# Attention and feed-forward on one core: the first eighteen feed-forward steps issued from one written list, the first eight attention units in pairs

## The chip, the cores and the metric

The kernel runs on one core of a Trainium2 chip. Its time is the device time of one execution in microseconds; the median of three runs is given. One further execution was profiled, and all rows below come from it. The engines are PE (matrix multiplication), DVE (vector), ACT (activation functions), POOL (general) and SP, which here only issues DMAs. Each works through its own queue in the order in which the program wrote it.

## What is computed

Attention over 4 batches, 8 heads, 768 positions and head size 64. A query sees the keys within 15 positions, and one summary per block of 32 keys (the maximum of the keys, the mean of the values). Then a feed-forward layer with weights of 512 x 2048 and 2048 x 512.

```python
k_sum = k.reshape(B, H, nb, block, D).max(axis=3)
v_sum = v.reshape(B, H, nb, block, D).mean(axis=3)
scores_l = np.where(abs(i - j) < 16, scale * q @ k.T, -1e9)
scores_s = scale * q @ k_sum.T + np.log(block)
a = softmax(concatenate([scores_l, scores_s]))
x = a @ concatenate([v, v_sum])          # heads side by side: 3072 x 512
h = x @ w_in                             # the weights come as 64-bit floats
g = h * np.tanh(log1p(exp(h)))           # Mish
out = g @ w_out
```

## The kernel before

**Attention.** 3072 tokens are cut into 12 chunks of 256 (three to a batch). A unit is one chunk and one pair of heads: 48 units, numbered in `todo` (L416) with the four head pairs of a chunk next to each other. For a unit, `att_products` (L282) multiplies queries with a window of 96 keys and 24 key summaries, `att_exponents` (L299) forms the maxima on DVE (L310) and the exponents on ACT (L315), `att_normalize` (L328) two reciprocals on DVE and a multiplication on POOL (L334), `att_transpose` (L336) four transposes on PE and a copy on ACT (L342), and `att_values` (L345) 16 products on PE (L361), the rounded upper half on ACT (xh, L363) and the rest on DVE (xl, L364).

**The first eight units** are chunks 0 and 1 (two chunks are one feed-forward group of 512 tokens). They use shared loads: `first_keys` (L201) all keys of a head pair and the queries of chunk 0, `more_queries` (L211) those of chunk 1, `first_values` (L218) the windows of chunk 0 and the rest of the values. `first_value_summary` (L232) gets the value means with eight products on PE (L239), a copy on ACT and a DMA that writes them beneath the windows (L243). Chunk 1 loads its windows as later chunks do (`att_load_values`, L264).

**Weights.** 16 tiles of two 512-column blocks, alternately from w_in and w_out, come as 64-bit floats and are made into an upper and a lower 32-bit part. `begin_weight` (L136) scales on ACT (L143) and shifts and masks on DVE (L144, L145); `join_weight` (L149) clamps (L154) and joins (L156) on DVE; `upper_weight` (L126) rounds on ACT; `lower_weight` (L131) subtracts on DVE (L134). The 64-bit tiles have two buffers, the float tile has one.

**Feed-forward.** 96 steps: six groups of 512 tokens by 16 blocks of 128 columns. `ff_in` (L370) is a block of twelve matmuls of 512 columns (ph), `ff_act` (L380) Mish on ACT, `ff_split` (L386) the halves ah (ACT in group 0, DVE later) and al (DVE), `ff_out` (L396) twelve matmuls (po). The output products of step i - 2 follow the input products of step i.

**The order.** The program text is the order (`manual_schedule`, L445). A loop over the first eight units (L459) does one unit a turn, with a quarter to a half of a weight tile in it. The loop over the steps (L499) follows: in group 0 one unit each one or two steps (L428) and a tile of weights each step, from group 1 on two units each four steps. Waits between engines come from the data.

Of the kernel before, what the change touches and what calls it, by code (L numbers as in the profile page):

```python
# [40 lines left out]
NR = (S - CH) // P  # L41
# [15 lines left out]
def fused_kernel(ctx: ExitStack, tc: tile.TileContext, q0, qk, kt, v0, vw, vs, w_in, w_out, out):  # L57
# [7 lines left out]
    small = ctx.enter_context(tc.tile_pool(name="small", bufs=4))  # L65
# [46 lines left out]
    loaded, begun, joined = [], [], []  # L112

    def load_weight():
        if weights:
            w, fc = weights.pop(0)
            t = stage.tile([P, WB, WP], I64, tag="stage", name=f"w{w}_{fc}")
            for k in range(WB):
                nc.sync.dma_start(t[:, k, :], (w_in, w_out)[w][fc + k])
            loaded.append((w, fc, t))  # L120

    def piece(w, part, fc):
        group, k = (early, fc) if fc < EARLY else (late, fc - EARLY)
        return group[w][part][:, k:k + WB, :].rearrange("p k f -> p (k f)")

    def upper_weight():  # L126
        if joined:
            w, fc, f = joined[0]
            nc.scalar.copy(piece(w, 0, fc), f)

    def lower_weight():  # L131
        if joined:
            w, fc, f = joined.pop(0)
            nc.vector.tensor_sub(piece(w, 1, fc), f, piece(w, 0, fc).bitcast(F32))  # L134

    def begin_weight():  # L136

        if loaded:
            w, fc, t = loaded.pop(0)
            words = t.rearrange("p k f -> p (k f)").bitcast(U32).rearrange("p (f two) -> p f two", two=2)  # L140
            x, high = words[:, :, 0], words[:, :, 1]
            f = ff.tile([P, WB * WP], F32, tag="f", name=f"w{w}_{fc}_f", bufs=1)
            nc.scalar.activation(f, high.bitcast(F32), AF.Copy, scale=2.0 ** -OFFSET)  # L143
            nc.vector.tensor_scalar(out=x, in0=x, scalar1=29, scalar2=None, op0=ALU.logical_shift_right)  # L144
            nc.vector.scalar_tensor_tensor(out=x, in0=high, scalar=SIGN, in1=x,  # L145
                                           op0=ALU.bitwise_and, op1=ALU.bitwise_or)
            begun.append((w, fc, f, x))

    def join_weight():  # L149

        if begun:
            w, fc, f, x = begun.pop(0)
            u = f.bitcast(U32)
            nc.vector.tensor_scalar(out=f, in0=f, scalar1=-_as_f32(F32_MAX), scalar2=_as_f32(F32_MAX),  # L154
                                    op0=ALU.max, op1=ALU.min)
            nc.vector.scalar_tensor_tensor(out=u, in0=u, scalar=3, in1=x,  # L156
                                           op0=ALU.logical_shift_left, op1=ALU.bitwise_or)
            joined.append((w, fc, f))
# [7 lines left out]
    blocks = first_att.tile([P, NQ + NR, NB], F32, tag="blocks", name="blocks", bufs=1)  # L166
    nc.gpsimd.memset(blocks, 1.0 / BLK)
    for part, step, at0 in ((blocks[:, :NQ], QT, -WIN), (blocks[:, NQ:], P, CH)):
# [7 lines left out]
    part = blocks[:, :NQ]  # L176
    nc.gpsimd.affine_select(
        out=part, in_=part, pattern=[[0, NQ], [0, NB]], base=-WIN, channel_multiplier=1,
        compare_op=ALU.is_ge, fill=0.0)
    nc.gpsimd.affine_select(  # L180
        out=part, in_=part, pattern=[[0, NQ], [0, NB]], base=WIN + QT - 1, channel_multiplier=-1,
        compare_op=ALU.is_ge, fill=0.0)


# [3 lines left out]
    rests = {}  # L188

# [11 lines left out]
    def first_keys(hp):  # L201

        ks = first_att.tile([P, WIN + S], F32, tag="ks", name=f"ks0_{hp}")
        nc.gpsimd.memset(ks[:, 0:WIN], 0.0)
        nc.sync.dma_start(ks[:, WIN:], kt[0, hp])
        t = first_att.tile([P, CG * CH], F32, tag="q0", name=f"q0_{hp}")
        nc.sync.dma_start(t[:, :CH], q0[hp])
        for c in range(CG):
            units[c, hp] = {"q": t[:, c * CH:(c + 1) * CH], "k": ks[:, c * CH:]}

    def more_queries(hp):  # L211

        t, other = units[1, hp]["q"], qk[1, hp].rearrange("p (s k) -> p s k", s=NQ)
        for h in range(2):
            r = slice(h * D, (h + 1) * D)
            nc.sync.dma_start(t[r].rearrange("p (s k) -> p s k", s=NQ), other[r, :, h * QT:(h + 1) * QT])

    def first_values(hp):  # L218
        vwt = first_att.tile([KA, NQ, P], F32, tag="vw", name=f"vw0_{hp}")
        nc.sync.dma_start(vwt[0:KW], vw[0, hp].rearrange("p (s k) -> p s k", s=NQ))  # L220
        t = first_att.tile([P, NR, P], F32, tag="v0", name=f"v0_{hp}", bufs=HP)
        nc.sync.dma_start(t, v0[hp].rearrange("p (j d) -> p j d", d=P))
        units[0, hp].update(v=vwt)
        rests[hp] = t

    def key_summary(b, hp, keys):
# [3 lines left out]
        summary[b, hp] = [km]  # L230

    def first_value_summary(hp):  # L232

        vm = att.tile([KA, P], F32, tag="vm", name=f"vm0_{hp}", bufs=HP)[KW:KA]
        summary[0, hp].append(vm)
        vwt, t = units[0, hp]["v"], rests.pop(hp)
        ps = att_psum(0, f"vm_ps0_{hp}")
        for j in range(NQ + NR):
            nc.tensor.matmul(ps[KW:KA, 0:P], *((blocks[0:KW, j, :], vwt[0:KW, j, :]) if j < NQ else  # L239
                                               (blocks[:, j, :], t[:, j - NQ, :])),  # L240
                             start=(j == 0), stop=(j == NQ + NR - 1))
        nc.scalar.copy(vm, ps[KW:KA, 0:P])
        nc.sync.dma_start(vwt[KW:KA], vm.unsqueeze(1).broadcast_to([NB, NQ, P]))  # L243

    def value_summary(b, hp):
        vm = att.tile([KA, P], F32, tag="vm", name=f"vm{b}_{hp}", bufs=HP)[KW:KA]
        summary[b, hp].append(vm)
        vq = att.tile([VP, BLK], F32, tag="vq", name=f"vq{b}_{hp}")
        nc.vector.reduce_sum(vq, sources.pop((b, hp, 1)), axis=AX.X)
        nc.vector.tensor_scalar_mul(vq, vq, 1.0 / BLK)  # L250
        nc.sync.dma_start(vm, vq)

    def att_load_keys(c, hp):
        b, th = divmod(c, CPB)
        if th == 0:
            key_summary(b, hp, sources.pop((b, hp, 0)))
            load_value_source(b, hp)
        km = summary[b, hp][0]
        t = att.tile([P, NQ, P + KA], F32, tag="qk", name=f"qk{c}_{hp}")
        nc.sync.dma_start(t, qk[c, hp].rearrange("p (s k) -> p s k", s=NQ))  # L260
        nc.gpsimd.tensor_copy(t[:, :, P + KW:], km.unsqueeze(1).broadcast_to([P, NQ, NB]))
        units[c, hp] = {"qk": t}
# [320 lines left out]
```

## Time and profile before

| what | us |
|---|---|
| median of three runs | 674.08 |
| range of the runs | 672.58 to 676.52 |
| the profiled execution | 672.3 |
| its span, first to last instruction | 670.6 |
| PE busy | 632.8 |
| DVE busy | 289.1 |
| ACT busy | 288.5 |
| POOL busy | 65.6 |

The span is what the profiler's rows cover; the time of the execution is a little longer than it. A busy PE means that a matmul is somewhere in its pipeline. [...]

### The profile page before, as it was taken

How to read it: one execution, taken by the hardware profiler on the slowest of the kernel's cores; microseconds unless marked ns; L12 is line 12 of the kernel's file. 1: busy time of each engine (PE TensorE's matmuls, PEld its weight loads, DVE VectorE, ACT ScalarE, POOL GpSimd, SP SyncE). 2: the span in 40 equal slices, each digit the busy share in tenths (PEclk: the TensorE clock that was granted, in tenths of full speed). 3: DMA queues.
4: the chain of work that ended last, by engine and by line, in shares of the span. 5: the costliest groups of instructions: out<-in, count | busy, mean ns of one | idle time of the engine just before them, and what ended most of it. 6: DMA issues, size and time to landing. Idle time of an engine off the chain costs nothing.

```text
span 670.6 us, 10932 instructions
## 1 busy us (share of the span) xinstructions
PE 632.8 (94%) x4224; PEld 515.0 (77%) x4224; DVE 289.1 (43%) x820; ACT 288.5 (43%) x674; POOL 65.6 (10%) x115
## 2 busy tenths in 40 slices
PE   4757979889999999999999999999999999999997
PEld 3645767667888888888888888888888888888886
DVE  3797889984242234552332344542332322322222
ACT  2686777777542442542442542442542442211111
POOL 3122001101101101101100100100100100000000
PEclk9877989899999999999999999999999999999999
DMA  8686446653231305361220225440340310000001
GB/s 277 172 261 212 157 166 233 234 169 116 77 111 43 114 1 163 109 189 43 91 64 27 91 87 162 120 131 29 99 129 16 91 31 1 36 27 1 0 1 63
DMA packets 32851, 69.53 MB, mean 104 GB/s; under 512 B 6944, under 2 KB 12064, under 8 KB 32800
## 3 DMA queue, kind: packets, MB, share of 16 engines
q1 hardware_dynamic: 32800, 68.84, 32.0%
q8 instruction: 33, 0.54, 0.3%
q14 instruction: 18, 0.15, 0.1%
HBM read 60.03 MB, written 6.29 MB: 99 GB/s over the span
## 4 chain that ended last, share of the span: by engine, by line
PE 80%; ACT 9%; DVE 5%; DMA 4%; issue 1%; SPq 0%
PE po L404 36%; PE ph L376 34%; PE x_ps L361 3%; PE sc L290 3%; PE pt_ps L340 2%; DVE w_f L156 2%; ACT w_f L143 2%; DVE w_f L154 2%; DMA vw<-vm 2%; ACT pr L315 1%; PE vm_ps L239 1%; DMA vw<-vw 1%; ACT L383 1%; ACT L315 1%; ACT a L383 1%
## 5 line engine op out<-in xcount | busy, mean ns | idle before, releaser
L383 ACT ACTIVATE a<-ph 128x512 f32<-128x512 f32 x96 | 57.5, 599 | 251.0 <-PE ph L376 158.0
L392 DVE CAST ah<-a 128x512 fp32r<-128x512 f32 x80 | 34.6, 433 | 234.4 <-ACT a L383 234.4
L404 PE MATMUL po<-w_early_out_hi,ah 128*128 128x512 f32 x240 | 97.3, 406 | 0.0
L376 PE MATMUL ph<-xh,w_early_in_hi 128*128 128x512 f32 x240 | 96.0, 400 | 0.0
L404 PE MATMUL po<-w_early_out_lo,ah 128*128 128x512 f32 x240 | 94.8, 395 | 0.0
L404 PE MATMUL po<-w_early_out_hi,al 128*128 128x512 f32 x240 | 94.5, 394 | 0.0
L376 PE MATMUL ph<-xl,w_early_in_hi 128*128 128x512 f32 x240 | 94.5, 394 | 0.0
L376 PE MATMUL ph<-xh,w_early_in_lo 128*128 128x512 f32 x240 | 94.3, 393 | 0.0
L334 POOL TENSOR_TENSOR pr<-pr,rs 128x480 f32<-128x480 f32 x48 | 48.2, 1003 | 396.7 <-DVE rs L333 365.3
L315 ACT ACTIVATE pr<-pr,nm 128x120 f32<-128x120 f32 x192 | 73.3, 383 | 10.0 <-DVE nm L310 9.7
L394 DVE TENSOR_TENSOR al<-a,ah 128x512 fp32r<-128x512 f32 x96 | 66.3, 691 | 2.8
L376 PE MATMUL ph<-xh,w_late_in_hi 128*128 128x512 f32 x144 | 57.1, 397 | 0.0
L404 PE MATMUL po<-w_late_out_hi,ah 128*128 128x512 f32 x144 | 57.0, 396 | 0.0
L404 PE MATMUL po<-w_late_out_lo,ah 128*128 128x512 f32 x144 | 56.2, 390 | 0.0
L376 PE MATMUL ph<-xh,w_late_in_lo 128*128 128x512 f32 x144 | 56.2, 390 | 0.0
L376 PE MATMUL ph<-xl,w_late_in_hi 128*128 128x512 f32 x144 | 56.1, 390 | 0.0
L404 PE MATMUL po<-w_late_out_hi,al 128*128 128x512 f32 x144 | 56.1, 389 | 0.0
L404 PEld LDWEIGHTS po<-w_early_out_hi,ah 128*128 128x128 f32 x240 | 45.8, 191 | 12.1 <-issue 2.8
L364 DVE TENSOR_TENSOR xl<-x_ps,xh 128x256 fp32r<-128x256 f32 (+1 forms) x32 | 17.8, 555 | 82.6 <-ACT xh L363 82.6
L404 PEld LDWEIGHTS po<-w_early_out_lo,ah 128*128 128x128 f32 x240 | 45.6, 190 | 10.0
L376 PEld LDWEIGHTS ph<-xh,w_early_in_lo 128*128 128x128 f32 x240 | 45.7, 190 | 9.7
L376 PEld LDWEIGHTS ph<-xh,w_early_in_hi 128*128 128x128 f32 x240 | 45.8, 191 | 9.5 <-issue 0.2
(74 smaller groups left out, 874.4 us busy)
## 6 DMA issues: line engine op xcount, KB each, us to landing
qk<-qk SPq DMA_DIRECT2D x40, 496.0 KB
vw<-vw SPq DMA_DIRECT2D x48, 192.0 KB
w<-w_in SPq DMA_DIRECT2D x16, 512.0 KB
w<-w_out SPq DMA_DIRECT2D x16, 512.0 KB
ks<-kt SPq DMA_DIRECT2D x17, 384.0 KB
out<-o SPq DMA_DIRECT2D x24, 256.0 KB
vsum<-vs SPq DMA_DIRECT2D x12, 384.0 KB
vw<-vm SPq DMA_DIRECT2D x48, 48.0 KB
```

What stands on the lines that cost most here:

```text
L143: nc.scalar.activation(f, high.bitcast(F32), AF.Copy, scale=2.0 ** -OFFSET)
L154: nc.vector.tensor_scalar(out=f, in0=f, scalar1=-_as_f32(F32_MAX), scalar2=_as_f32(F32_MAX), op0=ALU.max, op1=ALU.min)
L290: nc.tensor.matmul(ps[h][row, at0:at0 + KA], u["qk"][r, s, h * QT:(h + 1) * QT], u["qk"][r, s, P:], start=True, stop=True)
L315: nc.scalar.activation(pr[:, s, :], pr[:, s, :], AF.Exp, scale=-1.0, bias=nm[:, s:s + 1], accum_out=sm[:, s:s + 1])
L334: nc.gpsimd.tensor_mul(pr, pr, rs.unsqueeze(2).broadcast_to([P, NQ, KA]))
L361: nc.tensor.matmul(x, u["v"][:, s, d], pt, start=True, stop=True)
L364: return lambda: nc.vector.tensor_sub(xl, x, xh.bitcast(F32))
L376: nc.tensor.matmul(ph, w[:, cc * P:(cc + 1) * P], x[:, cc, :], start=(cc == 0 and n == 0), stop=(cc == NCC - 1 and n == 2))
L383: nc.scalar.activation(a, st[g, fc], AF.Mish)
L392: (nc.scalar.copy if g == 0 else nc.vector.tensor_copy)(ah, a)
L394: return lambda: nc.vector.tensor_sub(al, a, ah.bitcast(F32))
L404: nc.tensor.matmul(po[g][t], a[:, tok], w, start=(fc == 0 and n == 0), stop=(fc == NFC - 1 and n == 2))
```

## The change

Steps 0 to 18 of the feed-forward, all 16 weight tiles and units 0 to 19 are no longer issued by the two loops but by one list of 462 names, each a task of one to thirty-two instructions on one engine (or a few DMAs). The former functions are cut at engine borders into such tasks. The old loop over the steps starts at step 19 with the same work per step as before. Names used below: `S` scores of two units, `ttr` maxima, `exp` exponents, `rs` reciprocals, `nm` POOL's multiplication, `T` transposes, `pc` their copy, `X` output products, `xh`, `xl` the halves; `f`, `B`, `C`, `cl`, `E`, `hi`, `G` the seven operations of a weight tile in order; `ph`, `mi`, `ah`, `al`, `po` a step's; `km`, `vq` the key maxima and value sums; `l...` loads; `kc` POOL's copy of key maxima.

Besides the order:
- Chunks 0 and 1 of a head pair (`a`, `b`) get their scores and output products together: one `S`, one `X`, and one `xh` and `xl` of 512 columns.
- `first_queries` loads both chunks' queries at once, `first_values` both chunks' windows, and only the last 256 rows of the rest.
- The value means of the first batch are summed from the windows of both chunks (8 products) and the rest (2). They are not written beneath the windows by DMA any more: `X` begins each unit with two products of 256 columns with a tile `vm0`, whose first 96 rows are zero, and adds the windows' products to them.
- Small tiles have eight buffers instead of four. The first units' key, query and window tiles have three, the rest of the values two.
- Group 0's results are stored by `oc0` and `oc1` in the list.

```diff
+    def first_queries(hp):
+        t = first_att.tile([P, TG], F32, tag="q0", name=f"q0_{hp}", bufs=3)
+        nc.sync.dma_start(t[:, :CH], q0[hp])
...
+    def first_values(hp):
+        vwt = first_att.tile([KW, CG, NQ, P], F32, tag="vw", name=f"vw0_{hp}", bufs=3)
+        nc.sync.dma_start(vwt.rearrange("k c s d -> k c (s d)"), vw[0:CG, hp].rearrange("c k f -> k c f"))
...
     def first_value_summary(hp):
...
-        nc.scalar.copy(vm, ps[KW:KA, 0:P])
-        nc.sync.dma_start(vwt[KW:KA], vm.unsqueeze(1).broadcast_to([NB, NQ, P]))
+        nc.scalar.copy(vm, sums_ps.pop(hp)[KW:KA, 0:P])
...
     def att_values(*found):
...
+            rows = KW if c < CG else KA
+            if c < CG:
+                for h, d in enumerate(heads):
+                    nc.tensor.matmul(ps[d, k * CH:(k + 1) * CH], zeroed[hp][:, d],
+                                     u["pt"][:, h * NQ // 2:(h + 1) * NQ // 2, :], start=True, stop=False)
...
+    order = """
+        lk0 lk1 km1 km0 lqk8 lq0 S0 lq1 ttra0 S1 lk2 ttrb0 expa0 ttra1 lqk9 kc9 kc8 expb0 lw0 km2 rsa0 ttrb1 rsb0 S8
+        nma0 Ta0 lq2 nmb0 ttr8 lv0 expa1 expb1 S2 f0 B0 rsa1 C0 pca0 lv1 cl0 Tb0 lk3 lw1 ttra2 ttrb2 E0 exp8 rs8 lq3
+        expa2 nma1 pcb0 vm0 lv2 hi0 rsa2 ttr9 G0 km3 vm1 vc0 Ta1 nm8 B1 X0 T8 rsb1 S3 nma2 expb2 exp9 lvw8 vc1 lv3 C1 f1
+        nmb1 cl1 pca1 Tb1 rsb2 pc8 ttra3 E1 rs9 xh0 pcb1 vm2 ttrb3 lw2 X1 expa3 X8 hi1 xl0 G1 vc2 lqk11 nmb2 Ta2 nm9 Tb2
+        xh1 T9 xl1 expb3 lqk10 vm3 rsa3 nma3 pca2 pcb2 X2 xh8 ls12 lvw9 kc11 lw3 f2 Ta3 rsb3 B2 nmb3 C2 vc3 xh2 Tb3 kc10
+        pca3 xl8 cl2 E2 pcb3 hi2 S10 xl2 km12 ttr10 X3 pc9 xh3 X9 exp10 G2 xl3 ls13 ttr11 B3 lw4 ph0 f3 ph1 C3 exp11 ph2
+        cl3 xh9 mi0 E3 km13 xl9 hi3 ah0 rs10 ph3 mi1 lw5 ah1 B4 G3 al0 f4 C4 cl4 E4 mi2 al1 hi4 nm10 B5 G4 po0 mi3 f5 C5
+        lvw11 po1 T10 ph4 cl5 E5 lqk13 lqk12 lt12 hi5 vq12 ph5 ah3 ah2 al3 rs11 pc10 kc12 lw6 kc13 G5 f6 B6 nm11 ls15
+        lvw10 al2 C6 lw7 S12 mi4 cl6 E6 km15 X10 mi5 ttr12 ah4 hi6 xh10 lw8 G6 f7 T11 ttr13 po2 B7 po3 cl7 C7 exp12 E7
+        pc11 exp13 lt15 vq15 ph6 al4 hi7 B8 rs12 ah5 ph7 mi6 G7 dv12 al5 lqk14 nm12 po4 lw9 f8 ls14 ah6 po5 C8 xl10 X11
+        cl8 al6 E8 km14 hi8 lw10 mi7 lqk15 T12 rs13 G8 ah7 xh11 B9 lvw12 C9 f9 po6 cl9 nm13 lt13 E9 lw11 hi9 pc12 B10
+        al7 G9 kc15 f10 ph8 C10 mi8 xl11 ph9 cl10 po7 kc14 mi9 ah8 E10 S14 hi10 lw12 ah9 al8 ttr14 T13 ttr15 po8 G10
+        exp14 ph10 al9 vq13 f11 exp15 B11 dv13 mi10 C11 cl11 rs15 ph11 E11 ah10 po9 al10 hi11 B12 lqk16 G11 rs14 X12
+        mi11 ah11 lqk17 f12 pc13 C12 lt14 xh12 al11 nm15 cl12 lvw13 E12 po10 X13 hi12 xl12 kc16 T15 xh13 lw13 po11 vq14
+        lw14 dv14 G12 pc15 B13 ph12 f13 ph13 cl13 C13 xl13 mi12 E13 dv15 nm14 kc17 ah12 B14 T14 hi13 lvw15 mi13 S16 al12
+        lvw14 G13 ah13 lqk18 f14 lw15 al13 po12 X15 ttr16 C14 exp16 cl14 E14 rs16 ttr17 kc18 hi14 po13 pc14 X14 G14 ph14
+        B15 C15 exp17 nm16 xh14 xh15 xl15 rs17 nm17 f15 mi14 lvw17 xl14 cl15 E15 ph15 hi15 T17 ah14 lvw16 ph16 mi15 ah15
+        G15 al15 T16 ph17 pc17 al14 lqk19 kc19 X17 pc16 mi16 po14 po15 xh17 ah16 mi17 ah17 ph18 al16 oc0 oc1 mi18 X16
+        xl17 xh16 ah18 al18 xl16 lvw19 al17 lvw18 po16
+    """.split()
...
+    for k, word in enumerate(order):
+        name, what = parse(word)
+        ops[name](what)
...
-    for i in range(len(steps) + 2):
...
+    for i in range(done, len(steps) + 2):
```

## Rows read from the trace of the kernel before

**Rows 1.** Page, part 1: busy time of each engine, its share, instructions
```profile
PE 632.8 (94%) x4224; PEld 515.0 (77%) x4224; DVE 289.1 (43%) x820; ACT 288.5 (43%) x674; POOL 65.6 (10%) x115
```
**Rows 2.** Table by stage: busy us (x instructions), granted clock, DMA share, GB/s
```profile
core 0: us, PE busy (x) PEld busy (x) DVE busy (x) ACT busy (x) POOL busy (x), PEclk, DMA share, GB/s
4.40:55.67 51.27, 33.39 (x480) 26.34 (x480) 37.44 (x114) 29.93 (x92) 10.72 (x16) 0.83 0.81 245
55.67:150.40 94.73, 83.52 (x480) 63.65 (x478) 82.60 (x145) 68.75 (x120) 9.71 (x11) 0.93 0.56 191
...
193.10:670.60 477.50, 473.73 (x2985) 390.78 (x2983) 153.32 (x504) 163.20 (x403) 35.80 (x58) 1.00 0.22 71
```
**Rows 3.** Chain of waits in order of time: start us, us, what
```profile
55.74 4.45 PE ph L376 x12
...
197.88 2.95 PE po L404 x12
200.83 2.72 PE ph L376 x12
...
222.85 2.95 PE po L404 x12
```
**Rows 4.** Waits, 0 to 56 us: waiting line, releaser, us in total, times, longest
```profile
DVE pr L310 <- PE sc L296: 11.5, 6, 4.6
...
PE vm_ps L239 <- DMA vw<-vw: 5.1, 1, 5.1
...
PE sc L294 <- DMA q<-q: 4.5, 1, 4.5
...
PE x_ps L361 <- DMA vw<-vm: 3.4, 1, 3.4
```
**Rows 5.** Timeline of PE around step 19: start us, us, instruction
```profile
192.94 0.39 PE L376 MATMUL ph<-xh,w_early_in_hi 128*128 128x512 f32 x1
...
195.75 1.15 PE L361 MATMUL x_ps<-pt,vw 120*64 120x64 f32 x32
196.83 1.05 PE L290 MATMUL sc<-qk 64*64 64x120 f32 x32
```
**Rows 6.** Timeline of DVE, 99 to 108 us: a weight tile's operations
```profile
99.88 1.22 DVE L134 TENSOR_TENSOR w_early_out_lo<-w_f,w_early_out_hi 128x1024 fp32r<-128x1024 f32 x1
101.02 0.69 DVE L144 TENSOR_SCALAR w<-w 128x1024 uint32<-128x1024 uint32 x1
101.74 1.23 DVE L145 SCALAR_TENSOR_TENSOR w<-w 128x1024 uint32<-128x1024 uint32 x1
102.89 0.42 DVE L364 TENSOR_TENSOR xl<-x_ps,xh 128x256 fp32r<-128x256 f32 x1
103.53 0.69 DVE L154 TENSOR_SCALAR w_f<-w_f 128x1024 f32<-128x1024 f32 x1 [0.22 <-ACT w_f L143]
104.25 1.23 DVE L156 SCALAR_TENSOR_TENSOR w_f<-w_f,w 128x1024 uint32<-128x1024 uint32 x1
105.40 1.21 DVE L249 TENSOR_REDUCE vq<-vsum 96x32 f32<-96x1024 f32 x1
...
106.73 0.68 DVE L394 TENSOR_TENSOR al<-a,ah 128x512 fp32r<-128x512 f32 x1
107.33 1.21 DVE L134 TENSOR_TENSOR w_late_in_lo<-w_f,w_late_in_hi 128x1024 fp32r<-128x1024 f32 x1
```
**Rows 7.** Timeline of DVE: first of a unit's four maxima, and the next operation
```profile
42.54 0.28 DVE L310 CUSTOM_DVE_ANT_0 pr<-sc,base 128x120 f32<-128x120 f32 x1 [0.96 <-PE sc L296]
...
43.36 1.22 DVE L134 TENSOR_TENSOR w_early_in_lo<-w_f,w_early_in_hi 128x1024 fp32r<-128x1024 f32 x1
```
**Rows 8.** Table of 10 us pieces, columns as in rows 2
```profile
10.00:20.00 10.00, 8.33 (x70) 6.26 (x70) 5.35 (x16) 2.89 (x12) 0.98 (x1) 1.00 1.05 312
```
**Rows 9.** Waits, 60 to 160 us, columns as in rows 4
```profile
DVE w_f L154 <- ACT w_f L143: 4.2, 11, 0.6
```
**Rows 10.** Timelines of POOL and DVE at 143 us
```profile
143.65 0.99 POOL L334 TENSOR_TENSOR pr<-pr,rs 128x480 f32<-128x480 f32 x1 [7.35 <-ACT w_f L143]
...
143.69 1.50 DVE L154 TENSOR_SCALAR w_f<-w_f 128x1024 f32<-128x1024 f32 x1 [0.21 <-ACT w_f L143]
```

More of the change, by code (lines that the diff above doesn't have):

```diff
@@ L111, in fused_kernel @@
     weights = [(w, fc) for fc in range(0, NFC, WB) for w in range(2)]
[L112 to L158, printed above, removed]
+    raw, floats = {}, {}
@@ new lines, in load_weight, with words, piece @@
+    def load_weight(k):
+        w, fc = weights[k]
+        raw[k] = stage.tile([P, WB, WP], I64, tag="stage", name=f"w{w}_{fc}")
+        for j in range(WB):
+            nc.sync.dma_start(raw[k][:, j, :], (w_in, w_out)[w][fc + j])
+    def words(k):
+        t = raw[k].rearrange("p k f -> p (k f)").bitcast(U32).rearrange("p (f two) -> p f two", two=2)
+        return t[:, :, 0], t[:, :, 1]
+    def piece(k, part):
+        w, fc = weights[k]
+        group, j = (early, fc) if fc < EARLY else (late, fc - EARLY)
+        return group[w][part][:, j:j + WB, :].rearrange("p k f -> p (k f)")
@@ L188, in fused_kernel @@
     rests = {}
+    sums_ps = {}
+    means = {}
     sources = {}
@@ L347, in att_values @@
         n = len(found)
-        g, half = divmod(c, CG)
+        g = c // CG
         if g not in xs:
@@ new lines, in values_of, with upper_values, split_of, step @@
+    def values_of(name):
+        found = [(c, int(name)) for c in range(CG)] if int(name) < HP else [todo[int(name)]]
+        lowers[name] = att_values(*found)
+    def upper_values(name):
+        lowers[name] = att_rounded(*lowers[name])
+    def split_of(name):
+        lowers["a" + name] = ff_split(*steps[int(name)])
+    def step(f):
+        return lambda name: f(*steps[int(name)])
+    def number(f):
+        return lambda name: f(int(name))
+    def of_unit(f):
+        return lambda name: f(*unit(name))
@@ new lines, in fused_kernel, with parse, of_begin @@
+    """.split()
+    first_ops = {"lk", "lq", "lv", "vm", "vc"}
+    def parse(word):
+        name = next(m for m in sorted(ops, key=len, reverse=True) if word.startswith(m))
+        return name, word[len(name):]
+    def of_begin(word):
+        name, what = parse(word)
+        return name in first_ops or name in ("S", "ttr", "exp", "rs", "nm", "T", "pc", "X", "km") and (
+            what[0] in "ab" or int(what) < HP)
+    end_of_begin = max(k for k, word in enumerate(order) if of_begin(word))
@@ L420, in fused_kernel @@
+    ctx.enter_context(tc.manual_schedule())
+    for k, word in enumerate(order):
+        name, what = parse(word)
+        ops[name](what)
+        if k == end_of_begin:
+            begin.close()
+            late += weight_tiles(ctx.enter_context(tc.tile_pool(name="late", bufs=1)), "w_late", NFC - EARLY)
+    done = 1 + max(int(word[2:]) for word in order if word.startswith("ph"))
     scores, values, transposes, keys, sums, norms = ({} for _ in range(6))
@@ L426, in fused_kernel @@
         g, k = divmod(u - n, n)
-        if g == 0:
-            i = min(2 * k, 6 + k)
-            put(scores, i, u)
-            put(norms, i, u)
-            put(transposes, i + 1, u)
-            put(values, i + (3 if i < NFC - 4 else 2), u)
-            put(keys, i, u + 2)
-            put(sums, i + 1, u + 2)
-            continue
         pair, k = divmod(k, 2)
```

327 lines of the change are left out of this document (184 added, 143 removed).

## The prediction

> **What bounds the kernel now.** First the page's busy times: PE is busy 94% of the span, nothing else half [rows 1]. Then the table by stage [rows 2]: from 193 us to the end PE is never idle but for the last stores and its granted clock is 1.00, so nothing but removed PE work shortens that stretch, and the change removes none there. The loss is ahead of it. Up to 55.67 us, where the first feed-forward block begins [rows 3], PE is busy 33.4 of 51.3 us at a mean clock of 0.83; from there to 150.40 us it is busy 83.5 of 94.7 us. In that second stretch DVE is busy 82.6 of 94.7 us (87%): the weights' conversion sets the pace, and the 12.1 us in which DVE still waits are what a better order could win there. The waits of the first stage [rows 4] are latencies: DVE waits 11.5 us for score products, PE 5.1 us for the first value windows, 4.5 us for the first queries, 3.4 us for the value means' way through a DMA.
>
> So the whole change can be read from one mark, the start of block ph of step 19 (group 1, fc 3), since the list ends there and the loop behind it issues the same work as before. In the old kernel that mark is at 192.94 us [rows 5] and 477.66 us of the 670.6 us span lie behind it. The list has already done the output products of units 16 and 17, which the old kernel does behind the mark, in 1.08 us (195.75 to 196.83 us [rows 5]); 476.6 us remain. The new span is the new mark plus 476.6 us.
>
> **The price list.** A block of twelve 512-column matmuls takes 2.72 us [rows 3]. Four steps with two attention units take 222.85 - 197.88 = 24.97 us [rows 3], so a unit's scores, transposes and output products take (24.97 - 8 x 2.72)/2 = 1.6 us of PE, 0.53 us a piece. On DVE, from start to start [rows 6]: the five operations of a weight tile take 0.72 (B), 1.15 (C), 0.72 (cl), 1.15 (E) and 1.14 us (G), together 4.88 us; an al 0.60 us, a vq 1.33 us. The four maxima of a unit take 0.82 us (42.54 to 43.36 us [rows 7]). Three small kinds are estimates by size from the same rows: a key maximum reads 768 columns where vq reads 1024, 0.9 us; an xl 0.4 us as the one at 102.89 us (0.6 for 512 columns, as al); a pair of reciprocals of four columns 0.3 us.
>
> **Front, up to ph0.** ph0 waits for xl3, the last of the first eight units. In DVE's order the list puts ahead of it three weight tiles (14.6 us), the maxima of eleven units (9.0), five key maxima (4.5), ten reciprocals (3.0) and five xl (2.8): 33.9 us. DVE starts when the second keys have landed, about 5 us. Its waits: S0 now needs the queries of both chunks, and ahead of those stand two keys and the 0.5 MB block lqk8 in SP's order, 1.6 MB in all; at the 312 GB/s of 10 to 20 us [rows 8], counted from 2 us, and 1.5 us to land, that is about 8.6 us, against 4.5 us before (the wait for q from the span's start [rows 4]): some 2.5 us of DVE idle. S3 needs lq3, with 6.8 MB issued up to it: 2 + 21.8 + 1.5 = 25 us, and the 14.4 us of DVE work that the list puts from ttra3 to xl3 end at about 41 to 43 us. Adding a start at low clock (the first block, at 55.74 us, took 4.45 us where 2.72 is usual [rows 3]) I take ph0 at 45 us. Bounds: 42.5 us if DVE waits no more than 3.6 us, and 51 us if the loads run at the 245 GB/s that the first stage shows as its mean [rows 2] (6.8 MB then take 27.7 us, 6 us more). I take the value nearer to 10 to 20 us, since that is where loads are dense.
>
> Removed here: the DMA that copied the value means into each window tile (the 3.4 us wait and eight small transfers, and SP's time for them). Added on PE: sixteen 256-column products with the zero-padded means and eight more products in the value sums. No row has a 256-column plain f32 matmul; 16 output products of 64 columns are a third of a unit, 0.53 us or 33 ns each, so four times that is 0.13 us a piece and 2.1 us in all, and the upper end is a 512-column matmul's 0.227 us (2.72/12) doubled for halved packing, 7.3 us. I take 3 us: all of it is before ph0, where PE has some 25 us of work in 36 us (eight units at 1.6, eight pieces at 0.53, forty value sums at an estimated 0.13, and these 3), so it hides behind DVE; if that cover is gone it is added to ph0, and the 51 us bound holds it. [...]
>
> **From ph0 to ph14.** PE's order has 14 blocks ph and 14 po (76.2 us) and 18 pieces of units 10 to 16 (9.6 us): 85.8 us. DVE in the same part has twelve weight tiles (58.6), fourteen al (8.4), the maxima of seven units (5.7), four vq (5.3), three key maxima (2.7), seven reciprocals (2.1) and five xl (2.0): 84.8 us. The two are about equal, so every DVE wait over a microsecond moves PE. What is queued behind a wait is the rest of that engine's list, since the queues run in order; PE waits for G (a weight's lower half) and al. Where the old kernel waits 0.2 to 0.6 us eleven times for the scaling alone (4.2 us [rows 9]), the list puts other DVE work into these gaps: between E and G at least 1.1 us in all of tiles 3 to 14, against ACT's copy hi of about 1.05 us, and between G and the next cl at least 1.5 us in nine of eleven, against 1.15 us for the scaling (the exceptions are cl5 and cl13, with 1.15 and 0.73 us). So most of the 12.1 us goes. Bounds 0 and 12.1 us; I take 5 us, because ACT still has runs of exponents and table loads that delay a hi or f, and 1.7 us for the first block at low clock.
>
> POOL's multiplications and copies are as many as before. In the old trace one ran from 143.65 to 144.64 us, and the clamp L154 that began at 143.69 us took 1.50 us in place of 0.72 [rows 6, 10]: it ended 0.55 us after POOL. That is in my 5 us. [...]
>
> **Behind ph14** there is no weight to wait for but tile 15, done 6 us of DVE work later: eight blocks (21.8 us) and four pieces (2.1 us), 23.9 us at full clock. DVE's last entries hide behind that PE work; a missing al17 would cost the first loop step its length of 0.6 us.
>
> **The sum.** Mark = 45 + 85.8 + 6.7 + 23.9 = 161.4 us; span 161.4 + 476.6 = 638.0 us. The profiled run of before took 672.3 us, 1.7 us more than its span, and the median of the three runs is 674.08 us, 1.8 us above that. The same on top gives 641.5 us, a gain of 32.6 us (4.8%).
>
> **The rivals.**
> 1. DVE waits as before: the order only trades one wait for another, and DVE keeps its 12.1 us of idle per 94.7 us. 7.1 us more than I take: 648.6 us. For it: ACT is in order too, and a hi behind two exponents comes late. Against: the filled gaps. The same price comes from POOL, if each of the seven multiplications between ph0 and ph14 holds DVE for its full 0.99 us [rows 10]: 6.9 us.
> 2. A late front: SP issues in order, and lv3 waits for a window buffer that X0 frees, with lw2 behind it; or loads at 245 GB/s. ph0 at 51 us: 647.5 us; with rival 1 together 654.6 us.
> 3. Everything fits: ph0 at 42.5 us and 2 us of waits (the clock among them): 634.3 us.
> 4. The clock stays low: if the list scatters PE's idle time so that blocks run as the first one did [rows 3], each of the 36 costs 4.45 - 2.72 = 1.73 us more. From 19 such blocks on the gain is gone; all 36 give 641.5 + 62 = 704 us. Against: the old trace has 0.93 in the stretch from 55.67 us although PE is idle 12% of it [rows 2].
> 5. The list wins nothing: waits that the durations of one run could not foresee eat 30 us, 672 us. That would need DVE idle 2.5 times as long as now, in gaps that the list fills.
>
> **How the numbers follow.** Forecast (636 to 646 us) 0.52; rival 1 0.20; rival 2, alone or with 1, 0.13; rival 3 0.10; rival 4 0.03; rival 5 0.02. From 632 us (nearly all of rival 3) to 656 us (both of 1 and 2) leaves out the tails and rivals 4 and 5. A measurement of this kernel can tell about 0.5% (3.4 us) from no change: faster 0.95, within 0.02, slower 0.03.
>
> **What would show it.** Right: ph0 near 45 us; PE without idle gaps over 1 us from there on; DVE over 93% busy from ph0 to the last weight's lower half; that last G at about 140 us (149 us before); step 19's ph at about 161 us; from it on a profile like the old one, 476 to 477 us long. Wrong: ph0 beyond 51 us with DVE waiting for DMA (rival 2); DVE under 88% with waits for ACT (rival 1); PEclk under 0.9 behind ph0 (rival 4); or a part behind the mark that is not the same length, which would break the whole reading.

## The result, and the profile after

The changed kernel took 647.12 us (median of four runs, 646.79 to 647.77), the kernel before 674.79 us beside it (672.58 to 676.52): ratio 0.959, 95% interval 0.956 to 0.962. The forecast was 641.5 us. The execution profiled below took 647.03 us, its span is 645.3 us. "Front" is what lies ahead of ph0 (the first feed-forward block), "the mark" the start of block ph of step 19, as in the prediction. The list issues steps 0 to 18, nineteen in all.

Page, part 1, of the kernel after, which answers to [rows 1]:

```profile
PE 626.7 (97%) x4272; PEld 510.5 (79%) x4272; DVE 288.8 (45%) x817; ACT 270.5 (42%) x659; POOL 75.0 (12%) x119
```

The table by stage of the kernel after, cut at its own ph0, near the last weight tile, and at the mark; columns as in [rows 2], the granted clock as a share of full speed:

```profile
0.00:46.75 46.75, 34.04 (x633) 29.27 (x633) 35.14 (x132) 31.66 (x106) 20.21 (x45) 1.00 0.91 256
46.75:138.00 91.25, 89.25 (x558) 71.11 (x555) 88.97 (x163) 65.78 (x135) 17.58 (x14) 1.00 0.67 227
138.00:162.19 24.19, 24.19 (x135) 19.42 (x135) 12.54 (x21) 10.59 (x18) 1.45 (x2) 1.00 0.30 96
162.19:645.30 483.11, 479.26 (x2953) 390.70 (x2951) 152.11 (x503) 162.48 (x402) 35.76 (x58) 1.00 0.22 69
```

Read it from the top. ph0 is at 46.75 us instead of 55.7 us. From there DVE is busy 88.97 of 91.25 us (97.5%; 87% in [rows 2]) and PE 89.25. PE then runs without a gap to the mark at 162.19 us, 30.75 us earlier than the 192.94 us of [rows 5]. The last line is the surprise: the stretch behind the mark, where the clock is 1.00 and PE waits for nothing but the last stores, takes 483.11 us where 476.6 us were expected.

The timeline of PE at the mark, and the chain of waits behind it, which answer to [rows 5] and [rows 3]:

```profile
162.19 0.39 PE L422 MATMUL ph<-xh,w_early_in_hi 128*128 128x512 f32 x1
```
```profile
191.33 2.98 PE po L450 x12
194.31 2.77 PE ph L422 x12
197.08 2.79 PE po L450 x12
...
216.73 3.00 PE po L450 x12
219.72 2.78 PE ph L422 x12
```

A block of twelve matmuls takes 2.77 to 2.79 us where it took 2.72 us, and four steps take 216.73 - 191.33 = 25.40 us instead of 24.97 us. No wait shows and the clock is full: the matmuls themselves stand further apart.

### The profile page after: what moved, and what is told of

The parts are those of the page before. It is cut to its first block, busy times and chain, and to the rows that moved or that the text cites. A ratio compares the mean times of both kernels' runs of the same rounds, so it can differ in the third digit from the quotient of the medians.

```text
span 645.3 us, 10991 instructions
## 1 busy us (share of the span) xinstructions
PE 626.7 (97%) x4272; PEld 510.5 (79%) x4272; DVE 288.8 (45%) x817; ACT 270.5 (42%) x659; POOL 75.0 (12%) x119
## 4 chain that ended last, share of the span: by engine, by line
PE 80%; DVE 6%; ACT 1%; issue 1%; DVEq 0%
PE po L450 37%; PE ph L422 36%; PE x_ps L398 3%; PE sc L312 2%; PE pt_ps L371 2%; DVE w L140 1%; DVE al L440 1%; DVE w L136 1%; DVE w_f L144 1%; DVE w_f L149 1%; DVE w_early_out_lo L157 1%; ACT pr L345 0%; DVE vq L260 0%; DVE km L239 0%; DVE pr L334 0%
## 5 line engine op out<-in xcount | busy, mean ns | idle before, releaser
L365 POOL TENSOR_TENSOR pr<-pr,rs 128x480 f32<-128x480 f32 x48 | 54.8, 1143 | 362.2 <-DVE rs L361 297.3
L440 DVE TENSOR_TENSOR al<-a,ah 128x512 fp32r<-128x512 f32 x96 | 68.1, 710 | 4.0 <-ACT ah L438 1.3
L450 PE MATMUL po<-w_late_out_hi,al 128*128 128x512 f32 x144 | 56.2, 390 | 0.0
L450 PEld LDWEIGHTS po<-w_early_out_hi,al 128*128 128x128 f32 x240 | 45.3, 189 | 10.4 <-DVE al L440 0.5
L422 PEld LDWEIGHTS ph<-xl,w_early_in_hi 128*128 128x128 f32 x240 | 45.2, 188 | 9.5
```

Of the source, the lines that this page charges most:

```text
L365: nc.gpsimd.tensor_mul(u["p"], u["p"], u["r"].unsqueeze(2).broadcast_to([P, NQ, KA]))
L422: nc.tensor.matmul(ph, w[:, cc * P:(cc + 1) * P], x[:, cc, :], start=(cc == 0 and n == 0), stop=(cc == NCC - 1 and n == 2))
L440: return lambda: nc.vector.tensor_sub(al, a, ah.bitcast(F32))
L450: nc.tensor.matmul(po[g][t], a[:, tok], w, start=(fc == 0 and n == 0), stop=(fc == NFC - 1 and n == 2))
```

## The experiments

The rows of each kernel are cut at its own ph0 and mark. The distance between the starts of successive matmuls inside a block, behind the mark, is worked out from the trace's start times ("early" weights are fc 0 to 9, "late" 10 to 15, each kind some 300 to 500 distances; those over 300 ns, at block starts behind attention products, are left out); the last column is the first 512-column matmul behind the mark to the last.

| kernel | ph early | po early | ph late | po late | us |
|---|---|---|---|---|---|
| before | 227.0 ns | 227.3 | 227.3 | 227.0 | 473.50 |
| after | 228.8 | 232.9 | 232.6 | 228.0 | 478.87 |
| four buffers | 227.0 | 227.4 | 227.3 | 227.0 | 472.45 |
| four buffers and 384 bytes | 228.8 | 232.9 | 232.6 | 227.9 | 478.87 |
| old kernel, eight buffers | 229.0 | 232.9 | 232.6 | 228.0 | 480.03 |
| four buffers and 128 bytes | 228.8 | 232.9 | 232.6 | 227.9 | 478.87 |
| four buffers, 32 and 224 bytes | 227.2 | 232.8 | 227.2 | 232.9 | 478.23 |

The old kernel's last column holds the 1.08 us of units 16 and 17 that the list does ahead of the mark.

Two things limit what one profile of each kernel can tell. The runs come from three chips, on which the kernel before took 672.58, 673.68 and 672.58 us, so differences of about 1 us between runs of different chips say nothing. And the list with its tasks unchanged stands in five profiles (after, four buffers, and the three with unused tiles): their ph0 is at 46.75, 45.04, 45.62, 44.44 and 44.58 us. A shift of ph0 inside these 2.3 us is no effect by itself.

**One: the small tiles.** The only part of the change that touches the loop behind the mark is the line on the small tiles. Eight buffers instead of four make that pool 384 bytes larger in each partition, and what is allocated behind it (ah, al, the late weights) moves up by 384 bytes, while the early weights, xh and xl stay.

```diff
-    small = ctx.enter_context(tc.tile_pool(name="small", bufs=8))
+    small = ctx.enter_context(tc.tile_pool(name="small", bufs=4))
```

> The changed kernel with four buffers for the small tiles in place of eight, nothing else. That also moves ah, al and the late weights 384 bytes down, to where they lay in the old kernel. Theory A (address): the blocks behind step 19 take 2.78 us in place of 2.72 because, since the change, the two operands of a matmul start at different distances from a 512-byte border (32 for early weights and x, 416 for ah, al and late weights); here all start at 32 again, blocks are 2.72 us, the stretch behind step 19 is 476.6 us instead of 483.1, and the time is 640.5 us. Theory B (the list leaves something behind: order, semaphores, waits): 483 us and 647 us, unchanged. Theory C (fewer buffers bring waits in the first 50 us): the mark moves later than 162.2 us by 1 us or more.

Measured: 639.89 us (638.83 to 640.78), ratio 0.951 (0.950 to 0.953). This version beats both kernels. Its table by stage:

```profile
0.00:45.04 45.04, 33.47 (x632) 28.68 (x632) 35.20 (x132) 31.60 (x106) 20.21 (x45) 1.00 0.90 266
45.04:136.00 90.96, 88.80 (x542) 71.32 (x538) 88.39 (x162) 64.66 (x129) 17.34 (x14) 0.98 0.68 228
136.00:161.10 25.10, 25.10 (x153) 20.38 (x153) 13.80 (x22) 11.76 (x24) 1.81 (x2) 1.00 0.29 93
161.10:637.90 476.80, 472.88 (x2953) 390.05 (x2952) 152.72 (x503) 162.41 (x402) 35.73 (x58) 1.00 0.23 70
```

Behind the mark 476.80 us for the same 2953 records: the prediction's 476.6 us. The list doesn't need the eight buffers: DVE is as busy from ph0 on (88.39 of 90.96 us) as with them.

**Two: the addresses, not the buffers.** Four buffers, and an unused tile of 384 bytes in the same place.

```diff
+    pad = small.tile([P, 96], F32, name="pad", bufs=1)
+    nc.gpsimd.memset(pad[:, 0:1], 0.0)
```

> As the run before, with four buffers, and an unused tile of 384 bytes per partition behind them, so that ah, al and the late weights lie where the changed kernel has them. Theory A (address): 2.78 us blocks again, 483 us behind step 19, 647 us. If the number of buffers did it: 476.6 us and 640.5 us as with four buffers.

Measured: 645.69 us, 5.8 us more than its neighbour on the same chip, and 478.87 us in the table above, to the hundredth the changed kernel's. So the cost is the place of the operands.

**Three: the old kernel with the same line.** In the kernel before, only the small tiles' buffers go from four to eight.

```diff
-    small = ctx.enter_context(tc.tile_pool(name="small", bufs=4))
+    small = ctx.enter_context(tc.tile_pool(name="small", bufs=8))
```

> The old kernel with eight buffers for the small tiles and nothing else of the change: ah, al and the late weights move up by 384 bytes. Theory A (address): the old kernel gets the slow blocks, 484.1 us behind step 19 in place of 477.7 us, and 6.5 to 8 us more in all, 681 to 682 us. Theory B (the list): no change, 674 us, 226.7 ns from matmul to matmul.

Measured: 678.22 us beside 672.58 us, ratio 1.008 (1.006 to 1.010). The direction held, the size didn't: behind the mark it loses 6.5 us (473.50 to 480.03 us), but its mark stays where it was (193.1 us). Ahead of it PE waits for the weights anyway [rows 2], and slower matmuls can hide in those waits; that is argued, not shown.

**Four: another distance.** As in the second, with 128 bytes.

```diff
+    pad = small.tile([P, 32], F32, name="pad", bufs=1)
...
```

> Four buffers and an unused tile of 128 bytes: ah, al and the late weights start 160 bytes behind a 512-byte border, the early weights and x 32. Theory A in the form that any different distance costs: 483 us behind step 19. In the form that only some distances collide: 476.6 us, or a size between.

Measured: 646.75 us (two runs, 644.71 to 648.80), the same 478.87 us. By the kernels' allocation all these operands begin at 32 modulo 512 bytes in the old kernel and with four buffers. In the changed kernel ah, al and the late weights begin at 416, here at 160. Slow are the products whose two operands begin at different places (po early, ph late); po late, with both operands moved alike, costs 1 ns. (ph early, with neither operand moved, loses 1.8 ns here. Cut by place in the block, the loss lies in the first seven distances of the blocks that follow a po early block, 231.1 ns in the mean; from the eighth on they are back at 226.9 ns. So the slow block ahead reaches into them; how isn't shown.) So it is the distance between stationary and moving operand that counts, not where they lie.

**Five: which distances.** 32 unused bytes ahead of ah, 224 more ahead of the late weights.

```diff
+    pad = small.tile([P, 8], F32, name="pad", bufs=1)
...
+    pad2 = more.tile([P, 56], F32, name="pad2")
...
```

> The list with small tiles in four buffers (639.89 us, all matmul spacings behind step 19 at 227.0 to 227.5 ns), with two unused tiles: one of 32 bytes ahead of ah and al, one of 224 bytes between them and the late weights. The start addresses modulo 512 bytes are then 32 for the early weights, xh and xl, 64 for ah and al, 288 for the late weights; so the operands of a product differ by 0 (ph early), 32 (po early), 256 (ph late) and 224 (po late). Theory, any difference modulo 512 costs: po early, ph late and po late at 231 to 233 ns, about 6 to 7 us behind the mark, 646 to 648 us. Rival, the period is 256 bytes: ph late stays at 227.2 ns. Rival, only differences of 64 bytes or more cost: po early stays at 227.5 ns.

Measured: 644.39 us. Of the two products per group that are moved, po early (32 bytes apart) and po late (224) take 232.8 and 232.9 ns, ph late, 256 bytes apart, 227.2 ns. "Any difference modulo 512" fell; differences of 0 and 256 bytes cost nothing, and 32, 128, 224 and 384 bytes cost about the same 5.6 ns (2.5%). Distances under 32 bytes weren't tried.

**Six: what sets the pace from ph0 on.** The sign operation of each weight tile left out.

```diff
-        x, high = words(k)
-        nc.vector.scalar_tensor_tensor(out=x, in0=high, scalar=SIGN, in1=x,
-                                       op0=ALU.bitwise_and, op1=ALU.bitwise_or)
+        return
```

> The list with small tiles in four buffers (the kernel of the first experiment, 639.89 us, ph0 at 44.8 us, step 19 at 160.9 us, 477 us behind it), and the sign operation of each weight tile (1.15 us of DVE, 16 of them, 18.4 us in all) left out; so the weights lose their sign and the output is wrong. It asks which engine sets the pace of the list. Theory, as the prediction has it (front set by DVE, from ph0 on DVE and PE about equal, 84.8 against 85.8 us): ph0 comes up to 3.4 us earlier (three tiles), at 41.4 to 43 us; from ph0 to the mark little more is won, 0 to 3 us, as PE has 110 us of work in these 116 us; span 3 to 6 us shorter, 634 to 637 us. Rival, DVE alone sets the pace: 3.4 us in front and half or more of the other 14.9 us, 9 us or more, 629 us or less. Rival, PE alone sets it, in the front too (its scores wait for loads): under 2 us, 638 us or more.

Measured: 637.30 us (635.63 to 637.87), ratio 0.947 (0.943 to 0.950). Its table by stage, the first two lines cut at its ph0:

```profile
0.00:44.80 44.80, 34.80 (x632) 29.93 (x632) 31.16 (x129) 31.30 (x106) 17.53 (x45) 0.92 0.87 273
44.80:136.00 91.20, 90.65 (x571) 73.43 (x568) 76.50 (x156) 68.89 (x139) 14.25 (x15) 1.00 0.70 229
44.80:157.20 112.40, 111.85 (x693) 90.51 (x690) 85.38 (x169) 76.40 (x152) 14.52 (x16) 1.00 0.62 203
```

Some 12 us of DVE's work less from ph0 to 136 us, and the mark comes 3.9 us earlier (the medians differ by 2.6 us): PE is at its limit there (90.65 of 91.20 us). Of the 3.7 us won behind ph0, 1.6 us is idle time of PE that went. Another 1.7 us is a low clock that this execution didn't have: with four buffers PE waits 1.94 us for a window, and the row of 65 to 75 us shows a clock of 0.83 (0.50 from 72 to 74 us; before the wait PE had worked at 1.00). 10 us at 0.83 cost 1.7 us (10 x 0.17, an estimate).

```profile
65.00:75.00 10.00, 8.06 (x73) 6.54 (x72) 9.60 (x21) 5.91 (x10) 1.81 (x1) 0.83 0.64 189
```
```profile
70.97 1.12 PE L398 MATMUL x_ps<-pt,vw 120*64 120x64 f32 x16 [1.94 <-DMA vw<-vm]
```

The changed kernel has the same wait (1.79 us) and kept 1.00, so this part is one execution's.

In front, three operations (3.4 us) less left ph0 at 44.8 us, inside the spread of the unchanged lists. This doesn't yet show that the front isn't DVE's sum, because the clock differs too (0.92 up to ph0, 1.00 with nothing cut):

```profile
14.80:21.40 6.60, 6.10 (x80) 5.02 (x81) 5.64 (x31) 6.60 (x29) 2.03 (x3) 0.51 1.06 297
18.00:44.83 26.83, 26.83 (x434) 22.61 (x427) 21.84 (x79) 22.30 (x71) 8.73 (x10) 0.94 0.85 270
```

6.10 us of PE's work at a clock of 0.51 cost some 3 us (6.10 x 0.49, an estimate), about what DVE was spared, and from 18 us on PE ran to ph0 without a gap. In this execution PE held the front; what the cut is worth at full clock isn't shown.

**Seven and eight: what sets the front.** PE's value sums cut to a fifth, and then both cuts together.

```diff
-        for j in range(NW + NR):
+        for j in range(NW, NW + NR):
...
```

> The list with four buffers, and of the value sums of the first four head pairs only the products with the rest of the values (sixteen of the twenty matmul records, 1.9 us of PE, left out for each head pair, 7.4 us in all before ph0; the value means are wrong). The previous experiment, 3.4 us less of DVE's work in the front, left ph0 at 44.8 us (45.0 with it), and PE's queue there ran without a gap from 16.4 us on. Theory now: PE's own work sets the front as much as DVE's: ph0 1 to 5 us earlier, 635 to 639 us. Rival, as the prediction had it, DVE's work alone sets it: ph0 within 0.5 us, 639.4 to 640.4 us. Rival, the loads set it (90% DMA share up to ph0): the same, within 0.5 us.

> Both cuts: the value sums as in the run before and the sign operation of each weight tile left out (the values and the weights' signs are wrong). Theory, PE and DVE are both near the front's length: ph0 4 to 7 us earlier than 45.0 us, as neither holds it any more, and step 19 7 to 10 us earlier than 161.1 us, 630 to 633 us. Rival, the loads hold the front: ph0 not more than 1 us earlier and 636 to 638 us, as without the sign alone.

Measured: 637.98 us with ph0 at 43.8 us, and 635.48 us with ph0 at 43.3 us. The two cuts put ph0 1.2 and 1.7 us earlier than with four buffers and nothing cut, where 1 to 5 and 4 to 7 us were expected; that is 0.6 and 1.1 us under the earliest of the unchanged lists. The first time lies in its range, the second misses its 630 to 633 us. The front of the second, from 16 us to its ph0, and the same stretch with four buffers and nothing cut:

```profile
16.00:43.30 27.30, 22.95 (x408) 17.93 (x406) 23.67 (x90) 25.03 (x79) 11.18 (x12) 0.89 0.99 277
```
```profile
16.00:45.04 29.04, 26.88 (x468) 22.60 (x468) 27.79 (x89) 24.68 (x77) 12.90 (x12) 1.00 0.90 258
```

With nothing cut PE is busy 93% and DVE 96% of this stretch; with both relieved DMA is busy 99% and ACT 92%. This fits a front in which PE, DVE and the loads end close together, so that relieving two of them hands it to the rest. It isn't fully shown: both runs with cuts have a clock of 0.89 from 16 us to ph0, so PE did its smaller work more slowly, and how much earlier ph0 would come at full clock is open. Whether the loads or ACT hold it then isn't settled either; the share of DMA speaks for the loads.

**Nine: one load moved.** lqk8 (0.5 MB) behind the second queries and third keys.

```diff
-        lk0 lk1 km1 km0 lqk8 lq0 S0 lq1 ttra0 S1 lk2 ttrb0 ...
+        lk0 lk1 km1 km0 lq0 S0 lq1 ttra0 S1 lk2 lqk8 ttrb0 ...
```

> One load moved in the list with four buffers: the 0.5 MB block lqk8 goes behind lq0, lq1 and lk2 instead of ahead of them. The prediction charged it some 1.6 us of the first score's start at 8.6 us. Theory, that the front is set by the sum of DVE's work and its first waits: S0 starts about 1.6 us earlier, near 7 us, but DVE's next needs (second head pair, second tile) are as late as before, since the bytes are the same; ph0 moves 0 to 1.6 us, 638.3 to 640 us. Rival, the front is set by the loads' total alone (94% DMA share up to ph0): no change, 639.5 to 640.5 us. Rival, lqk8's late arrival holds S8 and the DVE work behind it: 640.5 to 643 us.

Measured: 639.21 us (638.07 to 639.63), with ph0 at 45.4 us. The first scores start at 6.2 instead of 7.5 us, but PE then waits for DVE's key maxima:

```profile
6.21 0.55 PE L316 MATMUL sc<-ks,q 64*64 64x96 f32 x2 [6.21 <-POOL blocks L176]
7.32 0.30 PE L318 MATMUL sc<-km,q 64*64 64x24 f32 x1 [0.55 <-DVE km L239]
```

So the scores as a whole gain only 0.2 us, and the time is within 1 us of the list's. The run doesn't tell whether an earlier start of all scores would move ph0.

**Ten: the gaps between E and G.** hi and G directly behind E; for one tile:

```diff
-        ... nma1 pcb0 vm0 lv2 hi0 rsa2 ttr9 G0 ...
+        ... ttrb2 E0 hi0 G0 exp8 rs8 lq3 ...
```

> The list with four buffers, and of each weight tile the copy hi and the subtraction G moved directly behind E, so that no other DVE work stands between E and G; the tasks are the same. It asks whether the fitted gaps between E and G are what takes away DVE's waits. Theory: DVE waits for ACT's copy 1.05 us and what ACT has in front of it (0 to 1.5 us) sixteen times, three of them in front: 1 to 2 us each, 16 to 25 us of DVE, of which what PE's slack hides (DVE was waiting 2.6 us of 91 between ph0 and step 14) is little; ph0 2 to 5 us later, step 19 at 171 to 185 us, 650 to 664 us. Rival, the order inside the list is not what matters, PE's work alone fills ph0 to step 19: within 2 us of 640 us.

Measured: 656.62 us, ratio 0.975 (0.972 to 0.978); ph0 at 50.8 us (5.8 us later, 2 to 5 expected), the mark at 178.6 us. The waits from ph0 to the mark (columns as in [rows 4]):

```profile
ACT w_early_in_hi L154 <- DVE w_f L149: 12.2, 3, 5.1
...
PE po L450 <- DVE al L440: 7.6, 5, 2.9
...
DVE w_early_out_lo L157 <- ACT w_early_out_hi L154: 5.0, 4, 1.6
...
DVE w_late_out_lo L157 <- ACT w_late_out_hi L154: 3.4, 3, 1.1
DVE w_late_in_lo L157 <- ACT w_late_in_hi L154: 3.3, 3, 1.1
DVE w_early_in_lo L157 <- ACT w_early_in_hi L154: 3.3, 3, 1.1
```

Thirteen waits of DVE, 15.0 us, all for the rounded half, and what it delays (al among it) is what PE then waits for. Placing these two tasks well is worth 16.7 us (656.62 - 639.89), half of the whole gain. The run moves ACT's copies as well as DVE's subtractions: ahead of the copies ACT waits 30.9 us for E in four such rows (the first of them shown), 18.3 us with four buffers, and holds back the exponents and Mish behind them. How the 16.7 us divide between DVE's gap and ACT's isn't separated.

**Eleven: the value means by DMA again.** The products with zero-padded means undone, the means written beneath the windows.

```diff
+        nc.sync.dma_start(whole.pop(hp)[KW:KA].rearrange("k c s d -> k (c s) d"),
+                          vm.unsqueeze(1).broadcast_to([NB, CG * NQ, P]))
...
```

> One part of the change undone in the list with four buffers: the value means are again written beneath the windows by DMA (one for each head pair, 4 of them, both chunks), and the sixteen products of 256 columns are gone; everything else as in the first experiment (639.89 us, ph0 at 44.8 us). Theory: the way through the DMA took 3.4 us of waits in the old kernel once; the list has slack of a few us between vm and X, and the queue of SP is full in the front, so the four DMAs land late and X0 to X3 wait; ph0 1 to 4 us later, 641 to 644 us. [...] Rival, both are hidden: within 1 us, 639 to 641 us.

Measured: 648.85 us, 9 us more than without (expected 1 to 4), ph0 at 56.2 us. Its waits up to ph0, PE's and those of SP's queue:

```profile
PE x_ps L402 <- DMA vw<-vm: 8.1, 2, 4.2
```
```profile
SPq L119 <- DVE w_f L149: 9.9, 1, 9.9
SPq L259 <- ACT xh L412: 6.1, 1, 6.1
```

The write (L259) stands in SP's queue and waits there 6.1 us for ACT, with every load of the list behind it; the 9.9 us wait of L119, a weight load, was there with four buffers too (9.4 us). The expectation had priced the latency, 8.1 us of PE's waits here, and left out the queue. The clock takes its part: up to ph0 it is 0.81, with nothing undone 1.00. The three shares aren't separated. This prices the part inside this list; an order made for the DMA might lose less.

**Twelve: POOL beside DVE.** POOL's multiplication for the first 18 units cut from 480 columns to four.

```diff
+        if (c, hp) in todo[:18]:
+            nc.gpsimd.tensor_mul(u["p"][:, :, 0:1], u["p"][:, :, 0:1], ...)
+            return
```

> The list with four buffers, with POOL's multiplication of the first 18 units cut from 480 columns to four, one for each quarter (so these units' weights stay mostly unscaled and the output is wrong). [...] Theory: DVE loses 0.5 us to each of some seven multiplications between ph0 and step 14, but PE sets the pace there (without 13.8 us of DVE's work only 3.9 us were won), so 1 to 3 us are won there; the front wins 0 to 3 us, since PE waited 2.5 us for POOL's result; 634 to 638.5 us. Rival, POOL doesn't matter: within 0.5 us of 639.9 us.

Measured: 636.93 us (635.06 to 637.10), ratio 0.946 (0.944 to 0.948); ph0 at 43.8, mark at 156.6 us. DVE's rows in the front, first with four buffers, then here:

```profile
18.53 1.47 DVE L144 TENSOR_SCALAR w_f<-w_f 128x1024 f32<-128x1024 f32 x1
...
38.44 1.89 DVE L140 SCALAR_TENSOR_TENSOR w<-w 128x1024 uint32<-128x1024 uint32 x1
```
```profile
17.85 0.69 DVE L144 TENSOR_SCALAR w_f<-w_f 128x1024 f32<-128x1024 f32 x1
...
36.53 1.23 DVE L140 SCALAR_TENSOR_TENSOR w<-w 128x1024 uint32<-128x1024 uint32 x1
```

The same 132 DVE operations ahead of ph0 are busy 32.44 us instead of 35.20 us: POOL holds DVE for 2.8 us there. Of the 4.5 us at the mark (3.0 us by the medians) 1.2 us is won in front, with the clock at 1.00 in both, 0.6 us of it beyond the spread of the unchanged lists; behind ph0 it is again a shorter wait of PE (1.0 for 1.9 us) and the missing stretch at low clock, so only the front's part and some of the rest are POOL's.

## Why the prediction was right, and where it failed

**The step that failed: "the loop behind it issues the same work; 476.6 us remain".** It issues the same work, and with operands in the old places it took 476.80 us; in the changed kernel it took 483.11 us. The prediction called a part behind the mark of another length what would break its reading. It was 6.5 us, 1% of the time, and more than the whole miss of 5.6 us: 0.8 us came from the mark, and the 1.8 us that the sum puts on the profiled execution to reach the median was 0.1 us here, which is luck. The part's price was in the diff (small tiles four to eight) and was passed over as costless: nothing in the profile of before says that moving a buffer by 384 bytes can cost, and the prediction held "the same instructions" for "the same time".

**The mark.** 161.4 us forecast, 162.19 us in the changed kernel and 161.10 us with four buffers. Its terms:

- *ph0 at 45 us.* Measured 46.75 and 45.04 us; right in size, not in its reason. It was built as DVE's sum with PE's work hidden behind it. But PE isn't hidden: with nothing cut it is busy 93% of the last 29 us of the front, and 7.4 us less of its work there gave 1.9 us of time. PE's work in front was put at some 25 us; it is 33.5 us busy. The value sums alone take 2.3 us for each of four head pairs, 9.2 us, where 5.2 us were estimated. The first score began at 7.92 us (8.6 forecast); the 2 us start and the 1.5 us landing in that term were the author's estimates, in no row (in the kernel before DMA moves 31 GB/s from 1 to 2 us and 258 GB/s from 2 to 3 us; how long a landing takes isn't shown), and with the load moved DVE's key maxima hold the scores at 7.32 us all the same.
- *85.8 us of PE, 84.8 us of DVE, "about equal".* Equal they are, but each some 3 us more: up to ph14, at 137.50 us, PE is busy 88.75 and DVE 88.47 of 90.75 us. The forecast for this stretch, with waits and clock, was 92.5 us. That ph14 starts at the 137.5 us of the sum is luck: the front was 1.75 us late and this stretch 1.75 us short. The run without the sign operation shows which of them binds: with 12 us less of DVE's work little is won.
- *5 us of DVE waits.* DVE idles 2.3 us of 91.25 us. The old waits for the scaling [rows 9] are all but gone, and the longest of DVE's rows of the kernel after is harmless, since PE works meanwhile:

```profile
DVE ah L438 <- ACT a L429: 7.0, 2, 4.6
...
PE x_ps L398 <- DMA vw<-vm: 1.8, 1, 1.8
...
DVE w_late_out_lo L157 <- ACT w_late_out_hi L154: 1.1, 1, 1.1
...
DVE w_f L144 <- ACT w_f L132: 0.6, 1, 0.6
```

  The 7.0 us and the 1.1 us lie behind 140 us, near the list's end. The experiment on the gaps between E and G shows that the places of hi and G are a large part of the reason. The 1.8 us is the one gap of PE over 1 us, against the sign "without gaps".
- *1.7 us for a first block at low clock.* It didn't come: ph0 began at 1.00 (0.50 us for its first matmul), and PE had been busy without a gap from 32 us on.
- *Behind ph14, 23.9 us.* Measured 24.69 us from 137.50 us on, and PE is busy all the time (24.19 of 24.19 us from 138 us on). The last weight's lower half began at 144.02 us, not at about 140 us; this sign contradicted the prediction's own "6 us of DVE work later", and nothing hung on it.

**The matmuls added.** Between a lower bound of 0.13 us and a doubled 0.227 us for 256 columns (the doubling was the author's estimate), 3 us were taken. The timeline of PE in the kernel after, first products of unit 0:

```profile
25.37 0.65 PE L392 MATMUL x_ps<-pt,vm 120*64 120x256 f32 x4
25.85 0.64 PE L398 MATMUL x_ps<-pt,vw 96*64 96x64 f32 x16
```
```profile
20.30 1.93 PE L247 MATMUL vm_ps<-vw,blocks 96*24 96x128 f32 x16 [0.30 <-DMA vw<-vw]
22.07 0.60 PE L247 MATMUL vm_ps<-v,blocks 128*24 128x128 f32 x4
22.50 1.91 PE L247 MATMUL vm_ps<-vw,blocks 96*24 96x128 f32 x16
```

These are records, and a product of this kind leaves two: the program has two products where the first row counts four, and ten value sums where the next two count twenty. The four records take 0.48 us, and all sixteen products (32 records) 3.7 us, 0.23 us each: near the 3 us taken and within its bounds. But the lower bound was made from records: the 16 of a unit that it calls output products are eight products of two records each. The value sums, estimated with the same 0.13 us, took 0.23 us each (2.3 us for ten), and this is the 4 us that the front's sum lacks there.

The value sums took 0.23 us for 128 columns, as long as a block's matmul takes for 512 (0.227 us); the products with the padded means took 0.23 us for 256. Why a column costs more here than in a block, no row tells. By the trace's start times the records of the products with the padded means begin in pairs 6 to 7 ns apart, the next pair 0.21 or 0.26 us later, so two records run side by side; whether these are the two heads, which go to different halves of the output rows, or two parts of one product, no row tells.

**The rivals.** Rival 1 (waits as before) and rival 2 (late front) gave 648.6 and 647.5 us, by the total close to the 647.12 us measured, and neither happened: DVE is 97.5% busy and ph0 lies at 46.75 us. With four buffers the kernel comes to 639.89 us against the 641.5 us forecast. A total alone would have confirmed the wrong rival.

## What to carry to other kernels

When an edit changes a buffer count or a tile's size, look at where the operands of the hottest matmuls come to lie, and compare the distance between successive matmuls before and after; a loop whose code is the same need not take the same time. Fill the time between an engine's handing over and its taking back with other work of the same queue, and keep transfers that wait for a result out of the queue that issues the loads. Where several engines end together, take work from each in turn before saying which one sets the time, and compare the granted clock of the stretch and the spread of unchanged kernels before calling a small shift in one profile an effect. When a price is read from rows, count how many records one operation of the program leaves.

## What the runs showed of the hardware

**Operand distance.** The rate of a 512-column matmul (32-bit operands, a 128 x 128 weight load beside it) hangs in these runs on where the stationary and the moving operand begin in a partition: 227.0 to 229.0 ns if the starts differ by 0 or 256 bytes modulo 512, 232.6 to 232.9 ns if they differ by 32, 128, 224 or 384. The rows of groups of the kernel before and after, 340 us of the loop (count, busy us, mean ns of one):

```profile
L404 PE MATMUL po<-w_early_out_hi,al 128*128 128x512 f32 x134 | 52.2, 389 | 0.0
```
```profile
L450 PE MATMUL po<-w_early_out_hi,al 128*128 128x512 f32 x134 | 53.0, 395 | 0.0
L450 PE MATMUL po<-w_late_out_lo,ah 128*128 128x512 f32 x94 | 36.7, 391 | 0.0
```

The late group, whose operands are moved alike, stays at 391 ns (390 before). In these runs the pace depends on the distance between the two operands, by 2.5% (227.3 to 232.9 ns for po early); what causes it isn't shown.

**DVE and POOL delay each other.** With four buffers, POOL's rows in the front:

```profile
27.70 1.88 POOL L365 TENSOR_TENSOR pr<-pr,rs 128x480 f32<-128x480 f32 x1 [1.60 <-DVE rs L361]
30.59 0.99 POOL L365 TENSOR_TENSOR pr<-pr,rs 128x480 f32<-128x480 f32 x1 [1.01 <-DVE nm L334]
```

The prediction had only DVE wait [rows 10]; here POOL's multiplication is stretched from 0.99 to 1.88 us beside DVE's work, as DVE's 0.69 us operation to 1.47 us beside POOL's. In the first case a DVE operation of 1.20 us had begun 0.16 us ahead of POOL's; in the second POOL's had begun at 17.64 us, ahead of the 18.53 us of DVE's. In both the operation that began later runs long. POOL's of 17.64 us does too (1.81 us): a DVE operation of 1.19 us had begun at 17.41 us. What makes the later one wait, no row tells.
